# Batch 0's v requested on GpSimd's queue, and batch 1's q transposed on TensorE: one change to a fused attention and MLP kernel

## The chip, the cores and the metric

The kernel runs on one core of a Trainium2 chip. A core has five engines that run side by side: TensorE (PE, with its weight loads as PEld), VectorE (DVE), ScalarE (ACT), GpSimd (POOL) and SyncE (SP), and 16 DMA engines that all queues share. The metric is the device time of one execution in microseconds. Before the change the median of three runs was 294.74 us (294.08 to 295.0).

## The reference

Inputs are q, k and v of 8 batches, 8 heads, 576 positions and 64 features, in float32, and the weights of one MLP.

```python
q_s = softmax(q, axis=-1)              # over the 64 features
k_s = softmax(k, axis=2)               # over the 576 positions
kv  = einsum('bhsd,bhse->bhde', k_s, v)
x   = einsum('bhsd,bhde->bhse', q_s, kv)   # then heads side by side: 4608 x 512
h   = x @ w_in                         # 512 -> 2048
g   = h + sin(alpha * h) ** 2 / alpha
out = g @ w_out                        # 2048 -> 512
```

## The kernel before, in words

Each batch of q, k and v comes as three loads of 128 partitions x 4 x 576 floats, into a pool of five staging buffers (`load`, L85). Partition groups hold even and odd heads; index `ii` (0 or 1) picks two of the four head columns, and a load with `halves=True` is two transfers, one for each `ii`. The 576 positions are 64 groups (partitions) of J = 9 rows j.

For a batch, `exp_q` and `exp_k` (L120, L124) make bfloat16 exponentials on ACT; `norm_q` (L133) sums on DVE and multiplies into the tile qn; `cast_v` makes the bfloat16 v, vb. `kv_mm` (L149) multiplies the transposed k by v, with a column of ones in vb that gives k's sums; `kv_norm` (L162) divides on DVE and writes the block-diagonal weights kbd. q has to be transposed: `q_transpose` (L178) does it on TensorE with an identity, and copies from PSUM; `q_transpose_dma` (L188) does it with DMA transposes from SP. `attn_chunk` (L211) multiplies kbd by the transposed q, and a copy puts the result into xT, the input of the MLP.

The MLP runs over 9 blocks of 512 tokens. For a block, 16 slots `ni` make 128 of the 2048 hidden columns each: `mm_h` (L222) does 4 matmuls into PSUM, `sine` (L238) takes the sine on ACT and squares it on ACT, POOL or DVE, `combine` (L249) writes g on DVE. The output matmuls `mm_o` (L253) follow, 64 for a block; block 0 has its own order, `o_quad` (L354), 64 steps of which the last 16 use the last quarter of w_out. `take(os, n)` emits the next n of them between other work. `evac_o` copies from PSUM and stores.

The order of all instructions on each engine is the order in which the program calls them (`manual_schedule`); a DMA request is an instruction on the engine that issues it, waits there in turn, and goes to that engine's queue (SP, ACT or GpSimd). Transfers that cast float32 weights to bfloat16 (`load_win` L104, `load_wout` L109) go on GpSimd's queue. The kernel holds those back: a copy named held (L317) on GpSimd waits for k's first half, and the requests stand behind it. The first 256 columns of w_in come another way: as float32 on SP's queue into a staging buffer (wf, L278), with two casts on GpSimd (L321).

The head of the program deals with batch 0 by hand: q, k, v and wf are requested on SP in that order (L270 to L280). Between block 0's output matmuls it prepares batch 1 (L398 to L420), with `load_batch(2)` at L406. `late` (L379) is a table of loads that are requested after a given slot of block 0; each load of batch 1 has a DVE copy as a gate.

Of the kernel before, what the change touches and what calls it, by code (L numbers as in the profile page):

```python
# [15 lines left out]
F32 = mybir.dt.float32  # L16
# [7 lines left out]
def kernel(  # L24
# [20 lines left out]
    J = 9  # L45
# [30 lines left out]
    def src_view(t, b):  # L76
        return t[b].rearrange("(i e) (p j) d -> (e p) i (j d)", e=2, j=J)
# [7 lines left out]
    def load(name, t, b, halves=False, eng=nc.sync, gate=None):  # L85

        st = stage.tile([128, 4, J, D], F32, name=f"st_{name}", tag="st")
        for ii in range(2) if gate else ():
            gate(st[:, ii, 0, 0:1], zero)
        view = src_view(t, b)  # L90
        flat = st.rearrange("p i j d -> p i (j d)")
        if halves:
            for ii in range(2):
                eng.dma_start(out=flat[:, ii::2], in_=view[:, ii::2])  # L94
        else:
            eng.dma_start(out=flat, in_=view)
        staged[name, b] = st

    def load_batch(b):
        load("q", q, b)  # L100
        load("k", k, b)
        load("v", v, b)

    def load_win(c0, c1):  # L104
        n = slice(c0, c1)
        for x in range(2):
            nc.gpsimd.dma_start(out=win[64 * x:64 * x + 64, :, n], in_=win_v[x][:, :, n])

    def load_wout(c):  # L109
        nc.gpsimd.dma_start(out=wout[:, 4 * c:4 * c + 4, :], in_=wout_v[:, 4 * c:4 * c + 4, :])  # L110
# [9 lines left out]
    def exp_q(b):  # L120
        A["qe", b] = att2.tile([128, J, 4 * D], BF16, name="qe")
        exp_to(A["qe", b], staged["q", b])

    def exp_k(b):  # L124
        A["ke", b] = att2.tile([128, J, 4 * D], BF16, name="ke")
        exp_to(A["ke", b], staged["k", b])

    def cast_v(b, engs):
        vv = vb[b % 2].rearrange("p j (i c) -> p i j c", i=4)
        for ii in range(2):  # L130
            engs[ii](vv[:, 2 * ii:2 * ii + 2, :, 0:D], staged["v", b][:, ii::2])  # L131

    def norm_q(b, engs):  # L133

        qe = A["qe", b].rearrange("p j (ii x d) -> p ii j x d", ii=2, x=2)
        A["qn", b] = qn = att1.tile([128, 2, J, 2 * D], BF16, name="qn")
        qs = small.tile([128, J, 4], F32, name="qs")
        if len(engs) == 1:
            nc.vector.tensor_reduce(qs, A["qe", b].rearrange("p j (i d) -> p j i d", i=4), axis=AXL.X, op=ALU.add)  # L139
            nc.vector.reciprocal(qs, qs)  # L140
        for ii in range(2):
            part = qs[:, :, 2 * ii:2 * ii + 2]
            if len(engs) == 2:
                nc.vector.tensor_reduce(part, qe[:, ii], axis=AXL.X, op=ALU.add)  # L144
                nc.vector.reciprocal(part, part)
            engs[ii % len(engs)].tensor_tensor(qn[:, ii].rearrange("p j (x d) -> p j x d", x=2), qe[:, ii],  # L146
                                               part.unsqueeze(3).to_broadcast([128, J, 2, D]), op=ALU.mult)

    def kv_mm(b, ii, pool, split=False):  # L149

        if ii == 0 or split:
            A["kvp", b] = pool.tile([128, 2, 512], F32, name="kvp", tag="a")
        kvp, ke, vt = A["kvp", b], A["ke", b], vb[b % 2]
        for j in range(J):
            for e in range(2):
                r = slice(64 * e, 64 * e + 64)
                nc.tensor.matmul(kvp[:, e, ii * 130:(ii + 1) * 130],  # L157
                                 ke[r, j, ii * 128:(ii + 1) * 128],
                                 vt[r, j, ii * 130:(ii + 1) * 130],
                                 start=(j == 0), stop=(j == J - 1))  # L160
# [17 lines left out]
    def q_transpose(b, ii, pool, eng):  # L178
        tp = pool.tile([128, 16, 128], BF16, name="tp", tag="a")
        q_transpose_ii(b, ii, 0, J, tp)  # L180
        eng(q_tile(b)[:, ii], tp[:, 0:J])
# [6 lines left out]
    def q_transpose_dma(b, halves=False):  # L188
        for ii in range(2) if halves else (slice(0, 2),):
            out, in_ = q_tile(b)[:, ii], A["qn", b][:, ii]  # L190
            if not halves:
                out, in_ = out.rearrange("p ii j c -> p (ii j) c"), in_.rearrange("p ii j c -> p ii (j c)")
                in_ = in_.rearrange("p ii c -> p (ii c)")
            else:
                in_ = in_.rearrange("p j c -> p (j c)")
            nc.sync.dma_start(out=out, in_=in_, transpose=True)
# [69 lines left out]

    ACT_CP, DVE_CP, GP_CP = nc.scalar.copy, nc.vector.tensor_copy, nc.gpsimd.tensor_copy
    V, GP = nc.vector, nc.gpsimd
    nc.scalar.dma_start(out=alpha_rows, in_=moe_alpha.rearrange("(no ni) -> no ni", ni=128))
    load("q", q, 0, halves=True)  # L270
    load("k", k, 0, halves=True)
    staged["v", 0] = st = stage.tile([128, 4, J, D], F32, name="st_v", tag="st")
    VJ = ((0, 0, 9), (1, 0, 5), (1, 5, 9))
    for ii, j0, j1 in VJ:
        nc.sync.dma_start(out=st[:, ii::2, j0:j1].rearrange("p i j d -> p i (j d)"),
                          in_=src_view(v, 0)[:, ii::2, j0 * D:j1 * D])

    wf = stage.tile([128, 4, J, D], F32, name="st_w", tag="st")[:, :, 0:4].rearrange("p c a b -> p c (a b)")  # L278
    for x in range(2):
        nc.sync.dma_start(out=wf[64 * x:64 * x + 64], in_=win_v[x][:, :, 0:256])  # L280
    make_identity(nc, ident)
    DVE_CP(identb, ident)
    zero = singles.tile([128, 1], F32, name="zero")
# [13 lines left out]
    DVE_CP(alpha_sb, tpa)  # L297
    nc.vector.reciprocal(inva_sb, alpha_sb)

    exp_q(0)  # L300
    exp_k(0)

# [10 lines left out]
    warm_up(7)  # L313
    norm_q(0, [V, V])
    q_tile(0)

    GP_CP(singles.tile([128, 1], F32, name="held"), staged["k", 0][:, 0, 0, 0:1])  # L317
    for c0, c1 in ((256, 512), (512, 1024), (1024, 1536)):
        load_win(c0, c1)
    for n in range(2):  # L320
        GP_CP(win[:, :, n * 128:n * 128 + 128], wf[:, :, n * 128:n * 128 + 128])  # L321
    load_win(1536, 2048)
    for c in range(2):
        load_wout(c)
    q_transpose_ii(0, 0, 0, 8, tps[0])
    ACT_CP(A["qT", 0][:, 0, 0:8], tps[0])
    cast_v0(0, 0, 5, ACT_CP)
# [39 lines left out]
    def take(it, n=1000):  # L367
        for _ in range(n):
            if next(it, 0) == 0:
                return  # L370
# [4 lines left out]
    with ES:  # L375
        def lent():
            return ps_e.tile([128, 2, MF], F32, name="hh", tag="a")[:, 0]

        late = {6: lambda: load("q", q, 1, halves=True, gate=DVE_CP), 8: lambda: load_wout(2),  # L379
                13: lambda: load("k", k, 1, halves=True, gate=DVE_CP)}  # L380
        for ki in range(2):
            for ni in range(2):
                mm_h(0, ni, lent, ki, ki + 1)
        for ni in range(nN):
            h_slot(0, ni, "DPAPPAPPAPPAPPAP"[ni], lag, lent)
            flush(lag, 1)
            if ni in late:
                late[ni]()
        flush(lag, 0)

        accs = [ps_h.tile([128, dm], F32, name="hp", tag="h") for _ in range(4)]
        os = o_quad(0, accs, [DVE_CP, ACT_CP, DVE_CP, ACT_CP])
        take(os, 20)
        xp = ps_e.tile([128, 4, P], F32, name="xp", tag="a")
        for c in range(4):
            attn_chunk(0, c, 8, 9, xp[:, c])
        DVE_CP(xT[:, :, 8 * P:9 * P], xp)
        take(os, 26)  # L398
        exp_q(1)
        load("v", v, 1, halves=True)  # L400
        norm_q(1, [GP, V])
        load_wout(3)
        exp_k(1)
        cast_v(1, [ACT_CP, DVE_CP])
        q_transpose_dma(1, halves=True)
        load_batch(2)  # L406
        nc.scalar.activation(zero, zero, AX.Sin)
        take(os, 2)
        for ii in range(2):
            kv_mm(1, ii, ps_e, split=True)  # L410
            kv_norm(1, ii, ii + 1)
        take(os, 4)

        c0 = J * P
        for ii in range(2):
            xp = ps_e.tile([128, 2, 512], F32, name="xp", tag="a")[:, :, 0:7 * P]
            for e in range(2):
                attn_chunk(1, 2 * ii + e, 0, 7, xp[:, e])
            (ACT_CP, DVE_CP)[ii](xT[:, 2 * ii:2 * ii + 2, c0:c0 + 7 * P], xp)
            take(os, 2)  # L420
        take(os)
        load("q", q, 3)
        load("k", k, 3)

        for ki in range(2):
            for ni in range(2):
                mm_h(1, ni, lent, ki, ki + 1)
        for ni in range(nN):
            h_slot(1, ni, SQ[ni], lag, lent)
            flush(lag, 1)  # L430
        cast_v(2, [GP_CP, GP_CP])
        flush(lag, 0)
# [134 lines left out]
```

## Time and profile before

| what | value |
|---|---|
| median of the runs | 294.74 us |
| profiled execution | 295.0 us |
| its span | 293.2 us |
| PE, ACT, DVE, POOL busy in the span | 275.7, 226.8, 188.0, 80.1 us |
| granted TensorE clock, mean | 0.993 |
| SP's queue | 42.28 MB, 48.1% of 16 engines' span |
| GpSimd's queue | 3.93 MB, 8.6% |
| first matmul of block 0, of block 1 | 16.29, 52.33 us |

Times in the views count from the start of the span. "Busy" of an engine is the time in its own instructions; a request for a DMA isn't counted. The chain that ended last goes back from the last instruction to whatever released it, step by step, and so shows which waits set the end. The bytes of GpSimd's queue are counted as written, in bfloat16; twice as many are read.

### The profile page before, as it was taken

How to read it: one execution, taken by the hardware profiler on the slowest of the kernel's cores; microseconds unless marked ns; L12 is line 12 of the kernel's file. 1: busy time of each engine (PE TensorE's matmuls, PEld its weight loads, DVE VectorE, ACT ScalarE, POOL GpSimd, SP SyncE). 2: the span in 40 equal slices, each digit the busy share in tenths (PEclk: the TensorE clock that was granted, in tenths of full speed). 3: DMA queues.
4: the chain of work that ended last, by engine and by line, in shares of the span. 5: the costliest groups of instructions: out<-in, count | busy, mean ns of one | idle time of the engine just before them, and what ended most of it. 6: DMA issues, size and time to landing. Idle time of an engine off the chain costs nothing.

```text
span 293.2 us, 4233 instructions
## 1 busy us (share of the span) xinstructions
PE 275.7 (94%) x1552; PEld 130.3 (44%) x1552; DVE 188.0 (64%) x279; ACT 226.8 (77%) x320; POOL 80.1 (27%) x74
## 2 busy tenths in 40 slices
PE   2799976999899999999999999999999999999995
PEld 1434442444445444444544454445444444444443
DVE  3867782599957847774767576766775455555412
ACT  4699862799748999889988998899887777777500
POOL 0678430466386646002420151005000000000000
PEclk9999997999999999999999999999999999999999
DMA  7999979993959986116941693115311111111142
GB/s 255 326 204 246 332 192 271 394 318 100 256 120 319 410 299 122 39 36 190 389 96 36 196 393 85 36 37 78 76 36 38 36 36 38 36 36 37 36 111 72
DMA packets 40261, 46.62 MB, mean 159 GB/s; under 512 B 18336, under 2 KB 23728, under 8 KB 40240
## 3 DMA queue, kind: packets, MB, share of 16 engines
q1 hardware_dynamic: 35760, 42.28, 48.1%
q0 software_dynamic: 4288, 3.93, 8.6%
q8 instruction: 12, 0.20, 0.3%
q10 hardware_dynamic: 192, 0.14, 0.2%
q14 instruction: 9, 0.07, 0.1%
HBM read 36.71 MB, written 9.44 MB: 157 GB/s over the span
## 4 chain that ended last, share of the span: by engine, by line
PE 82%; DMA 7%; DVE 3%; POOL 2%; issue 2%; SPq 1%; ACT 1%; POOLq 0%
PE hp L234 36%; PE op L254 33%; DMA st_w<-in_moe_w_in_dram 3%; PE hp L254 3%; PE hh L234 3%; DMA wout<-in_moe_w_out_dram 2%; PE kvp L157 2%; DMA qT<-qn 2%; PE xp L206 2%; DVE qs L144 1%; PE op L537 1%; PE op L234 1%; POOL s L244 1%; ACT s L240 1%; SPq L94 1%
## 5 line engine op out<-in xcount | busy, mean ns | idle before, releaser
L250 DVE SCALAR_TENSOR_TENSOR g<-s,inva_sb,hp 128x512 bf16<-128x512 f32 x130 | 96.2, 746 | 64.6 <-ACT s L242 54.2
L234 PE MATMUL hp<-xT,win 128*128 128x512 bf16 x520 | 129.9, 379 | 0.2 <-POOL win L321 0.2
L254 PE MATMUL op<-wout,g 128*128 128x512 bf16 x496 | 124.2, 379 | 0.0
L240 ACT ACTIVATE s<-hp,alpha_sb 128x512 f32<-128x512 f32 x130 | 87.7, 682 | 25.4 <-PE hp L234 24.2
L234 PEld LDWEIGHTS <-win 128*128 128x128 bf16 x576 | 56.2, 98 | 67.8 <-POOL win L321 0.9
L254 PEld LDWEIGHTS <-g 128*128 128x128 bf16 x560 | 54.5, 98 | 67.9 <-issue 7.4
L242 ACT ACTIVATE s<-s 128x512 f32<-128x512 f32 x112 | 70.5, 630 | 3.6
L146 POOL TENSOR_TENSOR qn<-qe,qs 128x1152 bf16<-128x1152 bf16 x12 | 25.3, 2128 | 72.3 <-DVE qs L140 62.4
L244 POOL TENSOR_TENSOR s<-s 128x512 f32<-128x512 f32 x29 | 30.5, 1063 | 27.1 <-ACT s L240 25.8
L260 DVE COPY o<-op 128x512 f32<-128x512 f32 (+2 forms) x33 | 22.1, 670 | 10.2 <-PE op L254 7.9
L117 ACT ACTIVATE qe<-st_q 128x1152 bf16<-128x1152 f32 x16 | 17.8, 1155 | 2.6 <-DMA st_q<-in_q_dram 2.5
L117 ACT ACTIVATE ke<-st_k 128x1152 bf16<-128x1152 f32 x16 | 17.9, 1151 | 2.5 <-DMA st_k<-in_k_dram 2.5
L254 PE MATMUL hp<-wout,g 128*128 128x512 bf16 x64 | 15.6, 397 | 4.0 <-DMA wout<-in_moe_w_out_dram 4.0
L139 DVE TENSOR_REDUCE qs<-qe 128x36 f32<-128x2304 bf16 x5 | 12.8, 2553 | 8.7 <-ACT qe L117 8.6
L131 POOL CAST vb<-st_v 128x1152 bf16<-128x1152 f32 x12 | 13.6, 1164 | 12.1 <-DMA st_v<-in_v_dram 7.9
L209 DVE CAST xT<-xp 128x512 bf16<-128x512 f32 (+1 forms) x18 | 13.4, 743 | 0.0
L157 PE MATMUL kvp<-vb,ke 64*128 64x130 bf16 x288 | 9.8, 216 | 0.8 <-ACT vb L310 0.8
L157 PEld LDWEIGHTS <-ke 64*128 64x128 bf16 x288 | 8.2, 93 | 4.1 <-issue 1.8
L117 ACT ACT_TABLE_LOAD x7 | 9.0, 1283 | 1.3 <-PEq L551 1.2
L234 PE MATMUL hh<-xT,win 128*128 128x512 bf16 x40 | 9.4, 379 | 0.0
L144 DVE TENSOR_REDUCE qs<-qe 128x18 f32<-128x1152 bf16 x6 | 8.0, 1330 | 1.9 <-ACT qe L117 1.9
L206 PE MATMUL xp<-qT,kbd 128*128 128x256 bf16 (+1 forms) x40 | 8.2, 286 | 0.4 <-DVE xT L209 0.3
(67 smaller groups left out, 114.6 us busy)
## 6 DMA issues: line engine op xcount, KB each, us to landing
out_dram<-o SPq DMA_DIRECT2D x70, 128.0 KB, 2.4
st_q<-in_q_dram SPq DMA_DIRECT2D x6, 1152.0 KB, 6.3
st_k<-in_k_dram SPq DMA_DIRECT2D x6, 1152.0 KB, 9.0
st_v<-in_v_dram SPq DMA_DIRECT2D x6, 1152.0 KB, 10.2
st_q<-in_q_dram SPq DMA_DIRECT2D x4, 576.0 KB, 5.4
st_k<-in_k_dram SPq DMA_DIRECT2D x4, 576.0 KB, 6.3
wout<-in_moe_w_out_dram POOLq DMA_DIRECT2D x4, 512.0 KB, 8.8
st_v<-in_v_dram SPq DMA_DIRECT2D x3, 576.0 KB, 8.0
```

Source lines behind the costliest of these rows:

```text
L117: nc.scalar.activation(dst[:, :, ii * 128:(ii + 1) * 128].rearrange("p j (x d) -> p x j d", x=2), src[:, ii::2], AX.Exp)
L131: engs[ii](vv[:, 2 * ii:2 * ii + 2, :, 0:D], staged["v", b][:, ii::2])
L146: engs[ii % len(engs)].tensor_tensor(qn[:, ii].rearrange("p j (x d) -> p j x d", x=2), qe[:, ii], part.unsqueeze(3).to_broadcast([128, J, ...
L157: nc.tensor.matmul(kvp[:, e, ii * 130:(ii + 1) * 130], ke[r, j, ii * 128:(ii + 1) * 128], vt[r, j, ii * 130:(ii + 1) * 130], start=(j == 0 ...
L206: nc.tensor.matmul(xp[:, e, 0:n], kt[:, e, ii], qT[:, ii, j0:j1, e * 64:(e + 1) * 64], start=True, stop=True)
L234: nc.tensor.matmul(hp, win[:, ki, ni * 128:(ni + 1) * 128], xT[:, ki, t * MF:(t + 1) * MF], start=(ki == 0), stop=(ki == 3))
L240: nc.scalar.activation(s, hp, AX.Sin, scale=alpha_sb[:, ni:ni + 1])
L242: nc.scalar.activation(s, s, AX.Square)
L244: nc.gpsimd.tensor_tensor(s, s, s, op=ALU.mult)
L250: nc.vector.scalar_tensor_tensor(G[t][:, ni], in0=s, scalar=inva_sb[:, ni:ni + 1], in1=hp, op0=ALU.mult, op1=ALU.add)
L254: nc.tensor.matmul(acc, G[t][:, ni, j * 128:(j + 1) * 128], wout[:, ni, :], start=(ni == 0), stop=(ni == nN - 1))
L260: eng(o[:, cols], acc)
```

## The change

- q of batch 0: the half `ii` = 0 is requested on SP, the half `ii` = 1 on ACT, and alpha's load comes behind that on ACT. k's halves stay on SP.
- The copy held waits for q's first half instead of k's. Behind it GpSimd requests v of batch 0 in the same three pieces, then all of w_in in five pairs (256, 256, 512, 512 and 512 columns), then two quarters of w_out.
- The float32 columns, wf, and their casts on GpSimd are gone.
- The last quarter of w_out is requested after slot 10 of block 0; it was requested after `norm_q(1)`.
- Batch 1's q is transposed on TensorE, with two copies on DVE, in place of two DMA transposes on SP. `load_batch(2)` comes right behind batch 1's v.
- Batch 1's `kv_mm` halves come after 8 and 2 more output matmuls; before they came after 2 more, one directly behind the other, with 4 behind them.

The words that came with the change also say that j 8 of batch 0 comes later; the diff holds nothing on that.

```diff
@@ head @@
+    staged["q", 0] = st = stage.tile([128, 4, J, D], F32, name="st_q", tag="st")
+    for ii, eng in ((0, nc.sync), (1, nc.scalar)):
+        eng.dma_start(out=st.rearrange("p i j d -> p i (j d)")[:, ii::2], in_=src_view(q, 0)[:, ii::2])
     nc.scalar.dma_start(out=alpha_rows, in_=moe_alpha.rearrange("(no ni) -> no ni", ni=128))
-    load("q", q, 0, halves=True)
     load("k", k, 0, halves=True)
-    staged["v", 0] = st = stage.tile([128, 4, J, D], F32, name="st_v", tag="st")
-    VJ = ((0, 0, 9), (1, 0, 5), (1, 5, 9))
-    for ii, j0, j1 in VJ:
-        nc.sync.dma_start(out=st[:, ii::2, j0:j1].rearrange("p i j d -> p i (j d)"),
-                          in_=src_view(v, 0)[:, ii::2, j0 * D:j1 * D])
-
-    wf = stage.tile([128, 4, J, D], F32, name="st_w", tag="st")[:, :, 0:4].rearrange("p c a b -> p c (a b)")
-    for x in range(2):
-        nc.sync.dma_start(out=wf[64 * x:64 * x + 64], in_=win_v[x][:, :, 0:256])
...
+    GP_CP(singles.tile([128, 1], F32, name="held"), staged["q", 0][:, 0, 0, 0:1])
+    staged["v", 0] = st = stage.tile([128, 4, J, D], F32, name="st_v", tag="st")
+    for ii, j0, j1 in ((0, 0, 9), (1, 0, 5), (1, 5, 9)):
+        GP.dma_start(out=st[:, ii::2, j0:j1].rearrange("p i j d -> p i (j d)"),
+                     in_=src_view(v, 0)[:, ii::2, j0 * D:j1 * D])
+    for c0, c1 in ((0, 256), (256, 512), (512, 1024), (1024, 1536), (1536, 2048)):
+        load_win(c0, c1)
+    for c in range(2):
+        load_wout(c)
...
-    GP_CP(singles.tile([128, 1], F32, name="held"), staged["k", 0][:, 0, 0, 0:1])
-    for c0, c1 in ((256, 512), (512, 1024), (1024, 1536)):
-        load_win(c0, c1)
-    for n in range(2):
-        GP_CP(win[:, :, n * 128:n * 128 + 128], wf[:, :, n * 128:n * 128 + 128])
-    load_win(1536, 2048)
-    for c in range(2):
-        load_wout(c)
@@ block 0 and batch 1 @@
         late = {6: lambda: load("q", q, 1, halves=True, gate=DVE_CP), 8: lambda: load_wout(2),
-                13: lambda: load("k", k, 1, halves=True, gate=DVE_CP)}
+                10: lambda: load_wout(3), 13: lambda: load("k", k, 1, halves=True, gate=DVE_CP)}
...
         load("v", v, 1, halves=True)
+        load_batch(2)
         norm_q(1, [GP, V])
-        load_wout(3)
         exp_k(1)
+        for ii in range(2):
+            q_transpose(1, ii, ps_e, DVE_CP)
         cast_v(1, [ACT_CP, DVE_CP])
-        q_transpose_dma(1, halves=True)
-        load_batch(2)
         nc.scalar.activation(zero, zero, AX.Sin)
+        take(os, 8)
+        kv_mm(1, 0, ps_e, split=True)
+        kv_norm(1, 0, 1)
         take(os, 2)
-        for ii in range(2):
-            kv_mm(1, ii, ps_e, split=True)
-            kv_norm(1, ii, ii + 1)
-        take(os, 4)
+        kv_mm(1, 1, ps_e, split=True)
+        kv_norm(1, 1, 2)
+        take(os, 1)
```

## The prediction

> **What bounds the kernel now.** I read the chain that ended last first (page part 4, then in order of time for the first 53 us), then the busy time by stage, then the timeline of the first 20 us, then the DMA requests. Over 82% of the chain is TensorE. What is not TensorE lies in two places that the change touches: before 16.85 us, and between 35 and 52 us.
>
> The chain of waits, in order of time (start, us, what):
> ```profile
> 5.39 10.09 DMA st_w<-in_moe_w_in_dram
> 15.62 1.19 POOL win L321 x2
> 16.85 1.69 PE hp L234 x7
> ...
> 37.25 2.07 POOL qn L146
> 39.32 6.91 DMA wout<-in_moe_w_out_dram
> 46.28 1.28 PE hp L254 x4
> 47.55 0.75 PE xp L214 x2
> 48.30 0.85 PE hp L254 x2
> 49.15 0.75 PE xp L214 x2
> 49.90 2.43 PE hp L254 x10
> 52.33 0.86 PE hp L234 x4
> ```
> The fourth quarter of w_out is requested at 39.32, because the request stands behind qn on GpSimd, and TensorE waits for it until 46.28. After that the matmuls are slow: 2 in 0.85 us at 48.30, where 16 took 3.45 us at 20.26 (0.2157 each).
>
> Busy time by stage (length, then busy of PE, PEld, DVE, ACT, POOL, granted clock, DMA share, GB/s):
> ```profile
> 16.85:30.62 13.77, 13.77 (x64) 6.28 (x65) 9.98 (x17) 13.26 (x22) 11.94 (x14) 1.00 1.21 242
> 30.62:41.03 10.41, 10.41 (x53) 4.61 (x51) 8.34 (x13) 8.77 (x9) 4.54 (x4) 1.00 0.97 291
> 41.03:52.33 11.30, 7.30 (x58) 3.60 (x58) 4.50 (x10) 2.31 (x4) 0.00 (x0) 0.85 1.03 242
> ```
> TensorE is full from 16.85 to 41.03, then has 7.30 us of 11.30, at a clock of 0.85. DVE, ACT and POOL are far from full there.
>
> The timeline of the head (start, us; in brackets the idle time before it and what ended it):
> ```profile
> 4.76 1.16 ACT L117 ACTIVATE qe<-st_q 128x1152 bf16<-128x1152 f32 x1 [2.25 <-DMA st_q<-in_q_dram]
> 5.95 1.35 DVE L144 TENSOR_REDUCE qs<-qe 128x18 f32<-128x1152 bf16 x1 [1.92 <-ACT qe L117]
> 6.17 1.16 ACT L117 ACTIVATE qe<-st_q 128x1152 bf16<-128x1152 f32 x1 [0.26 <-DMA st_q<-in_q_dram]
> 8.23 0.82 POOL L317 COPY held<-st_k 128x1 f32<-128x1 f32 x1 [6.92 <-DMA st_k<-in_k_dram]
> 8.99 4.07 POOL L107 DMA_DIRECT2D win<-in_moe_w_in_dram  x6
> 13.79 0.62 ACT L310 CAST vb<-st_v 128x512 bf16<-128x512 f32 x1 [1.46 <-DMA st_v<-in_v_dram]
> ```
> q's halves land near 4.7 and 6.1, v's last piece near 13.75. DVE's softmax chain (5.95 to 11.96) runs behind the first q half. A request on GpSimd's queue is slow to start: by the packet records, the first w_in data moved at about 13.2, 4.2 us after its request at 8.99; wout's last quarter, alone on the engines, reached its full rate 3.1 us after 39.32.
>
> **Part 1, the head: q on two queues, v and w_in on GpSimd's.** Removed: the two w_in requests on SP (0.75 each) and two casts on POOL (1.19 together, on the path at 15.62). Added: on ACT one q request (about 0.45, ahead of a table load with 2.25 idle behind it: free), and alpha behind it; on POOL three v requests and two more of w_in at about 0.65, with the wait for q in front.
>
> When does q land? Both halves are now asked for at 0.73 and the same 16 engines serve both. Where two queues were busy together, from 42.4 to 45.2 (wout and the transposes), each moved 37 to 40 packets in every 0.25 us, so I take one to one: both halves land at 6.1, the time of the second now. The bounds are 4.7 and 6.1. Then exp starts at 6.1 instead of 4.76, and all of DVE's chain moves by 1.35, from 11.96 to 13.3. alpha lands with q, near 6.3; its small transpose and two DVE operations (0.17 and 0.25) fit before 7.3.
>
> v: held ends at 6.1 + 0.82 = 6.95, data 3.1 to 4.2 later at 10.05 to 11.15 (k is through by 9.6), and 1.18 MB at about 400 GB/s (q's halves landed 1.45 apart, 0.59 MB each) with 0.3 for the last landing: v complete at 13.4 to 14.5, near the 13.75 of now. w_in's first 256 columns follow at 14.8 to 16, no cast behind them.
>
> From 13.3: ten transposes 0.73 (14.05), kvp of the first half 0.6 (14.7), of the second 0.6 (15.3; DVE's two v casts, 1.04, end at 14.25 and ACT's last one at 14.1 to 15.1), kvr and kbd 0.8 each on DVE (15.55, 16.35), the last two attention matmuls 0.61 (17.0), DVE's last xT 0.68 behind its own neighbour (17.75; now 17.10). Five of the 64 matmuls of block 0 are done by then; 59 x 0.2157 = 12.7 more end at 30.5, against 30.62. **Head: -0.1**, between +0.7 (v at the late end) and -1.2 (q's first half at 4.7 as now: the last xT near 16.4, end 29.3).
>
> The Trainium skill (DMA: Bandwidth & Descriptors, Specifications) gives about 1 us as first-byte latency on GpSimd's path. The rows here say 3.1 to 4.2, and the rows decide; with 1 us v would land near 12, and the sum would be the same, DVE's chain being last.
>
> Behind it: w_in's five pairs and w_out's two quarters stand in one queue, 6.3 MB at 400 GB/s. 128 columns come every 0.65 us and are used every 0.86, so block 0 does not starve. POOL's ninth request and those after wait for landings eight back, the last one near 17; POOL's first square comes at 19.5, so 2 us cover that.
>
> **Part 2, w_out's last quarter ten slots earlier.** It is requested after the squares of slots 9 and 10, near 28.9, in place of 39.32. Cost: 0.80 on POOL, whose squares of 12 and 13 come 0.5 later; the accumulators that wait for slot 13 are used 1.7 us into the next stage: at most 0.2. DMA: from 33 on, about 1.55 MB of w_out and 2.36 MB of k and v of batch 1 share 400 GB/s: w_out through by 41, v by 42.8 (now 40.74). That ends the wait of 46.28 - 42.2 = 4.0 us, and the slow clock after it.
>
> **Part 3, batch 1's q transposed on TensorE.** Removed: two DMA transposes that hold SP for 6.37 us and keep batch 2's loads until 45.87. Added: 18 transposes (ten took 0.73: 1.3) and two DVE copies of 128x1152 from PSUM. No row has that copy: ACT's 128x1024 took 0.99 (scaled 1.12), DVE's 128x896 cast from f32 1.09 (scaled 1.40); I take 1.25.
>
> **The stage from 30.62, walked.** TensorE: 46 output matmuls and j 8 until 40.5, as now. qn's halves are ready at 39.4 and 40.6: transposes to 41.85; 8 output matmuls to 43.55; kvp first half 44.15; 2 to 44.6; kvp second 45.2; 1 to 45.4. DVE: two copies 41.2 to 43.7, v cast 0.76 (44.5; v landed at 42.8), o 0.69 (45.2), norms 0.8 each (46.0, 46.8). The second pair of xp, 0.4 at full clock, then ends at 47.25 and five output matmuls at 48.3. Block 1 starts at 48.3 against 52.33: **-4.0**, from -3.4 to -4.6 with the copies at 1.40 and 1.12 and the transfers 1 us late or early. What is late next is DVE's kbd, not DMA.
>
> Batch 2's loads move past the transposes on SP, to about 33, behind v of batch 1 in the same queue. The four output tiles are stored behind them, near 52; their buffers are needed again only at 65. From block 1 on the order is unchanged and everything moves along; the DMA transposes of batch 2 (4.74 us on SP at 74.40) remain.
>
> **Sum.** Span 293.2 - 0.1 - 4.0 = 289.1. The profiled execution took 295.0, 1.8 more than its span: 290.9. It lies 0.26 above the median of the runs, 294.74: **290.6 us**. "j 8 of batch 0 later" is in the words but not in the diff; I cost it at nothing.
>
> **Rivals.**
> (a) q's first half still lands first, at 4.7: the head gains 1.2 in all and the time is 289.4. For it: each half is 16 descriptors for each engine, asked for by SP first. Against: the one-to-one packets above. The Trainium skill (the same page, Queues, rings and completion order) has each engine drain a packet of some 9 to 17 descriptors before it switches, by which this is what would happen; the rows of 42.4 to 45.2 do not show such bursts. Chance 0.13.
> (b) v comes late, 1 to 2 us after 13.75, since its request waits for q and POOL's copy: the head loses 0.7 to 2, 292.0. For it: 4.2 us on the first w_in request. Chance 0.20.
> (c) Slower: GpSimd's queue serves v like its slowest rows. w_in's longest landing was 9.3 us, w_out's 10.9. From 6.95 v's first piece then lands at 16.3 to 17.9, the last 1.5 to 2 later, at 18 to 20, and block 0 starts 4.3 to 6 us late: 294.9 to 296.6. It reaches no change and then decides from v complete at about 18.7, 5 us after now. Against: those rows had a backlog in front, v has none. Chance 0.12, 0.11 of it past the 0.3%.
> (d) The wait moves: batch 1's k and v are pushed back by w_out and kvp waits for them, 1 us for each us that v lands after 43.5. For no change v would have to land near 47.5; 294.5. The rates above leave no room for this. Chance 0.06.
> The forecast, 289.7 to 291.5: 0.49.
>
> **How the numbers follow.** A change of under 0.3% (0.9 us) can't be told from none. Slower is most of (c): 0.11. Same is (d) and the rest of (c): 0.07. Faster is the remainder: 0.82. The range takes in (a), (b) and the milder half of (d), and leaves out (c): 288.6 to 294.0.
>
> **What will show it.** Right: no wait for wout in the chain near 40 to 46; granted clock 1.00 in that stage; block 1's first L234 near 48.3; transposes right behind the 46th output matmul; exp of both q halves back to back from 6.1; first h matmul near 16.5. Wrong: ACT's or DVE's v cast after 15 with TensorE idle before kvp; TensorE waiting on win or on ke or vb of batch 1; clock below 1.00 in block 0.

## The result, and the profile after

| what | before | after |
|---|---|---|
| median of the runs compared, us | 294.87 (294.08 to 295.08, 4 runs) | 289.62 (289.56 to 289.95, 4 runs) |
| profiled execution, its span, us | 295.0, 293.2 | 289.56, 287.8 |
| block 0's first h matmul (L234), in the timeline | 16.29 | 16.79 |
| block 1's start (first long L234 piece of the chain) | 52.33 | 48.42 |
| from there to the end of the span | 240.9 | 239.4 |
| mean granted TensorE clock | 0.993 | 1.00 |

The ratio is 0.9829, with a 95% interval of 0.9809 to 0.9849: the changed kernel takes 1.7% less. Of the 5.4 us that the span loses, 3.9 lie ahead of block 1 and 1.5 behind it.

The chain of waits of the changed kernel, in order of time (start, us, what):

```profile
1.27 5.18 DMA alpha_rows<-in_moe_alpha_dram
...
7.08 0.25 DVE inva_sb L291
7.33 1.22 DVE qs L144
...
13.25 0.73 PE tp L186 x10
13.98 0.64 PE kvp L157 x18
...
33.27 10.52 DMA st_v<-in_v_dram
43.81 0.76 DVE vb L131
...
45.30 0.28 DVE kbd L170
45.60 0.30 DVE kbd L170
45.95 0.55 PE xp L214 x2
46.50 0.43 PE hp L254 x2
...
48.42 3.45 PE hp L234 x16
...
72.02 3.84 DMA qT<-qn
```

wout is gone from it. What stands there now is the second half of batch 1's v, which was requested at 33.27 and landed at 43.79; behind it come DVE's cast, its kbd and the last matmuls of block 0, at the granted clock of 1.00 (2 L254 in 0.43, against 0.85 before). The head of the chain begins with alpha's load, not with q: it comes behind q's second half on ACT's queue, and DVE's two operations on alpha end at 7.33, where DVE's first sum of q starts.

Busy time by stage of the changed kernel (length, then busy of PE, PEld, DVE, ACT, POOL, granted clock, DMA share, GB/s):

```profile
16.85:30.62 13.77, 13.77 (x65) 6.17 (x64) 10.17 (x17) 13.41 (x22) 9.68 (x11) 1.00 1.20 240
30.62:41.03 10.41, 10.39 (x54) 4.73 (x53) 8.34 (x12) 5.99 (x8) 4.50 (x4) 1.00 1.14 302
41.03:48.42 7.39, 7.32 (x78) 3.89 (x76) 5.25 (x12) 5.21 (x6) 0.00 (x0) 1.00 1.04 408
```

The stage that had 7.30 us of TensorE work in 11.30 us, at a clock of 0.85, now has 7.32 in 7.39, at 1.00. The DMA engines are as full in it as before by their share (1.04 against 1.03), but they move 408 GB/s in place of 242.

The timeline of the changed kernel (start, us; in brackets the idle time before it and what ended it):

```profile
5.80 2.22 ACT L117 ACTIVATE qe<-st_q 128x1152 bf16<-128x1152 f32 x2 [2.71 <-DMA st_q<-in_q_dram]
5.83 0.19 POOL L294 COPY held<-st_q 128x1 f32<-128x1 f32 x1 [4.51 <-DMA st_q<-in_q_dram]
5.95 2.32 POOL L297 DMA_DIRECT2D st_v<-in_v_dram  x3
...
13.25 0.73 PE L186 MATMUL tp<-identb,qn 128*128 128x128 bf16 x10 [0.67 <-DVE qn L146]
...
40.89 1.17 PE L186 MATMUL tp<-identb,qn 128*128 128x128 bf16 x18
41.59 1.42 DVE L181 COPY qT<-tp 128x1152 bf16<-128x1152 bf16 x2 [0.61 <-PE tp L186]
...
43.81 0.76 DVE L131 CAST vb<-st_v 128x1152 bf16<-128x1152 f32 x1 [0.80 <-DMA st_v<-in_v_dram]
```

q's two halves land at 5.77 (SP) and 6.23 (ACT), and exp of both runs back to back from 5.80. TensorE's transposes at 13.25 wait for DVE's qn, not for v. In batch 1, the two copies from PSUM take 1.42 us together, and then DVE stands for 0.80 us until v is there.

### The profile page after: what moved, and what is told of

Its sections match the earlier page's. It is cut to its first block, busy times and chain, and to the rows that moved or that the text cites. A ratio compares the mean times of both kernels' runs of the same rounds, so it can differ in the third digit from the quotient of the medians.

```text
span 287.8 us, 4258 instructions
## 1 busy us (share of the span) xinstructions
PE 275.4 (96%) x1570; PEld 130.8 (45%) x1570; DVE 188.6 (66%) x281; ACT 226.5 (79%) x320; POOL 81.7 (28%) x77
## 4 chain that ended last, share of the span: by engine, by line
PE 76%; DMA 7%; DVE 6%; ACT 4%; POOL 3%; issue 2%; ACTq 0%; SPq 0%; POOLq 0%
PE hp L234 34%; PE op L254 33%; DMA st_v<-in_v_dram 4%; POOL s L244 3%; ACT s L240 3%; PE kvp L157 2%; DMA alpha_rows<-in_moe_alpha_dram 2%; DVE qs L144 2%; PE xp L206 2%; DMA qT<-qn 1%; PE op L534 1%; PE op L234 1%; PE hh L234 1%; DVE qn L146 1%; DVE o L260 1%
## 5 line engine op out<-in xcount | busy, mean ns | idle before, releaser
L234 PE MATMUL hp<-xT,win 128*128 128x512 bf16 x520 | 129.8, 379 | 0.0
L254 PE MATMUL op<-wout,g 128*128 128x512 bf16 x496 | 124.2, 379 | 0.0
L234 PEld LDWEIGHTS <-win 128*128 128x128 bf16 x576 | 56.2, 98 | 67.4 <-issue 0.4
L254 PEld LDWEIGHTS <-g 128*128 128x128 bf16 x560 | 54.1, 98 | 61.7 <-issue 0.9
L254 PE MATMUL hp<-wout,g 128*128 128x512 bf16 x64 | 15.1, 379 | 0.0
L209 DVE CAST xT<-xp 128x512 bf16<-128x512 f32 (+1 forms) x18 | 13.4, 743 | 0.0
L234 PE MATMUL hh<-xT,win 128*128 128x512 bf16 x40 | 9.4, 379 | 0.0
```

What stands on the lines that cost most here:

```text
L234: nc.tensor.matmul(hp, win[:, ki, ni * 128:(ni + 1) * 128], xT[:, ki, t * MF:(t + 1) * MF], start=(ki == 0), stop=(ki == 3))
L254: nc.tensor.matmul(acc, G[t][:, ni, j * 128:(j + 1) * 128], wout[:, ni, :], start=(ni == 0), stop=(ni == nN - 1))
```

## The experiments

The kernel before varies more from run to run than the changed one: over the chips of the experiments its runs that are compared went from 293.56 to 297.90, those of the changed kernel from 289.42 to 290.64. Each ratio below is against runs of the kernel before on the same chip, and stands with its 95% interval; it is the measure to go by, since a difference from the median of all runs before on the chip can be off from it by more than 1 us.

**1. The head alone** (q on two queues, v and all of w_in on GpSimd's queue, no float32 columns; nothing else changed).

```diff
+    for ii, eng in ((0, nc.sync), (1, nc.scalar)):
+        eng.dma_start(out=st.rearrange("p i j d -> p i (j d)")[:, ii::2], in_=src_view(q, 0)[:, ii::2])
...
+    GP_CP(singles.tile([128, 1], F32, name="held"), staged["q", 0][:, 0, 0, 0:1])
+    for ii, j0, j1 in ((0, 0, 9), (1, 0, 5), (1, 5, 9)):
+        GP.dma_start(...)
```

> The head alone on the kernel before (q on two queues, v and w_in on GpSimd's). Theory: the head is worth nothing: q's first half lands a microsecond late and DVE's chain with it, the missing f32 columns and casts give that back. First output matmul of block 0 between 30.4 and 30.8 (before 30.46), time 294.4 to 295.2. Rival: the head carries 1 us or more of the gain, 293.9 or less.

Measured: 295.04 us (294.44 to 297.4), ratio 0.9988 [0.9944, 1.0032]. The head alone is worth nothing that can be measured, as the theory said, and the first output matmul of block 0 came at 30.58, inside the 30.4 to 30.8 expected. Its profiled execution was its slowest one (297.4), so its terms say less; the excess was not in the head: the chain there shows batch 1's DMA transposes at 9.57 us from 39.53.

**2. w_out alone** (the last quarter requested after slot 10; the DMA transposes stay).

```diff
-                13: lambda: load("k", k, 1, halves=True, gate=DVE_CP)}
+                10: lambda: load_wout(3), 13: lambda: load("k", k, 1, halves=True, gate=DVE_CP)}
...
-        load_wout(3)
```

> The last quarter of w_out requested after slot 10 and nothing else changed; DMA transposes kept. Theory: the wait for w_out (4.0 us) and the slow clock go, but w_out pushes batch 1's v to about 43.7, and the transposes land near 45 to 46; block 1 starts at 49.2 to 49.6, time 291.8 to 292.3. Rival 1: the request's place is the whole gain of the middle, block 1 at 48.4, 290.9. Rival 2: the DMA transposes hold the stage as long as w_out did, gain under 1.5 us, 293.4 or more.

Measured: 293.55 us (292.75 to 294.98), ratio 0.9892 [0.9819, 0.9965]. By the ratio that is 3.2 us gained, with an interval of 1.0 to 5.3; against the median of all runs before on that chip (295.21) it is 1.7. The time is that of the second rival (293.4 or more), but the chain holds v of batch 1 and kvp, not the DMA transposes. Block 1 starts at 51.49, against 52.33 before and 49.2 to 49.6 expected. The timeline and then the stage, of the kernel with this edit alone:

```profile
38.19 1.16 ACT L117 ACTIVATE ke<-st_k 128x1152 bf16<-128x1152 f32 x1 [3.09 <-DMA st_k<-in_k_dram]
40.49 1.16 ACT L117 ACTIVATE ke<-st_k 128x1152 bf16<-128x1152 f32 x1 [1.14 <-DMA st_k<-in_k_dram]
41.77 1.17 ACT L131 CAST vb<-st_v 128x1152 bf16<-128x1152 f32 x1
42.99 2.21 PE L157 MATMUL kvp<-vb,ke 64*128 64x130 bf16 x36 [2.78 <-ACT vb L131]
```

```profile
41.03:51.49 10.46, 8.28 (x56) 4.36 (x57) 4.76 (x10) 4.77 (x6) 0.00 (x0) 0.67 1.15 299
```

The wait on wout is gone, and another has come in its place: w_out's transfer now runs beside k of batch 1, ACT waits 3.09 and 1.14 us for k, and TensorE stands 2.78 us before kvp, which comes directly behind two output matmuls. The clock falls to 0.67. The changed kernel covers the same wait with TensorE work: its 18 transposes (1.17) and 8 output matmuls (1.89) stand ahead of kvp.

**3. TensorE transposes alone** (with the new order and batch 2's loads early; w_out stays late).

```diff
         load("v", v, 1, halves=True)
+        load_batch(2)
         norm_q(1, [GP, V])
         load_wout(3)
         exp_k(1)
+        for ii in range(2):
+            q_transpose(1, ii, ps_e, DVE_CP)
         cast_v(1, [ACT_CP, DVE_CP])
-        q_transpose_dma(1, halves=True)
-        load_batch(2)
...
```

> Batch 1's q transposed on TensorE, the loads of batch 2 and the order of the output matmuls as in the change, but the last quarter of w_out still requested behind qn on GpSimd, near 39.3. Theory: TensorE stops at the third of the eight output matmuls until w_out lands near 45; block 1 starts near 50.5, time 292.5 to 293.5. Rival: the transposes are what mattered, block 1 at 48.4 to 49, 290.9 to 291.5.

Measured: 298.25 us (297.59 to 298.85), ratio 1.0077 [1.004, 1.0114]: slower than before by 0.8%, against the expectation's sign. The chain of this kernel:

```profile
38.83 10.37 DMA wout<-in_moe_w_out_dram
...
57.25 3.45 PE hp L234 x16
```

w_out's last quarter, requested at the same time as before, takes 10.37 us to land in place of 6.91, and block 1 starts 4.9 us later. By the order of requests it is batch 2's loads, 3.5 MB that are now asked for ahead of it, that share the engines with it. That is a reading until something else is held fixed, so:

**4. The same, with batch 2's loads held back** behind a DVE copy until about 43 us.

```diff
-        load_batch(2)
...
+        load("q", q, 2, gate=DVE_CP)
+        load("k", k, 2)
+        load("v", v, 2)
```

> The kernel of the third experiment (q of batch 1 transposed on TensorE, w_out's last quarter still requested behind qn) with the loads of batch 2 held by a DVE copy behind v's cast, near 43.7, so that they don't share the engines with w_out. Theory: those loads are what made w_out take 10.4 us from its request and that kernel slower than before; here w_out lands near 45, block 1 starts at 50.5 to 51.5, time 291.5 to 293.0. Rival: w_out is as late without them, block 1 near 57, 297.5 or more.

Measured: 293.0 us (291.13 to 293.42) against 295.66, ratio 0.9891 [0.9848, 0.9934], at the upper end of what was expected. The chain:

```profile
38.81 5.80 DMA wout<-in_moe_w_out_dram
44.65 2.72 PE hp L254 x6
...
52.07 3.45 PE hp L234 x16
```

w_out lands 4.6 us sooner, and block 1 starts 5.2 us sooner. So it was batch 2's early loads that made experiment 3 slow, not the transposes on TensorE. The parts don't add: by the ratios, the head alone gives -0.4 us, w_out early -3.2, and the transposes with batch 2's early loads +2.3 (each known to 1.1 to 2.2 us either way), a sum of -1.3 where all three together gave -5.0. As these runs read, the early loads do no harm once w_out is ahead of them, and w_out's early transfer costs nothing once TensorE has work ahead of kvp.

**5. q of batch 0 on one queue**, in the changed kernel: both halves on SP, alpha first on ACT. (These are two changes: q's second half moves, and alpha no longer waits behind it.)

```diff
+    nc.scalar.dma_start(out=alpha_rows, ...)
-    for ii, eng in ((0, nc.sync), (1, nc.scalar)):
+    for ii, eng in ((0, nc.sync), (1, nc.sync)):
```

> The changed kernel with both halves of q on SP, alpha alone on ACT. Theory: exp of the first half starts at 4.7 in place of 5.8, DVE's chain (7.25 to 13.2) ends about 1.0 earlier and block 0 with it: 288.4 to 288.9. Rival 1: v, requested a microsecond earlier, then takes k's share and k is late: no change, 289.4 to 289.9. Rival 2: v or w_in's first columns bind at once, gain under 0.5.

Measured: 288.98 us (288.75 to 289.39), ratio 0.9737 [0.9684, 0.979]. In its profile v of batch 0, landed at 13.25, was the last thing ahead of kvp. To compare it with the changed kernel itself, both were run again on another chip, with one more edit beside them (experiment 6).

> The changed kernel as it is, timed beside the variants on one chip: 289.4 to 290.0.

> The changed kernel with q's halves both on SP, again, beside the changed kernel on one chip. Theory from its first profile: block 0 starts 1.0 earlier, but v of batch 1 lands only 0.4 earlier and block 1 starts 0.4 earlier; 0.3 to 0.7 faster than the changed kernel. Rival: the difference of the first run was between chips, under 0.2.

Measured there: the changed kernel 289.86 (289.42 to 290.64), q on one queue 289.13 (289.04 to 289.34), 0.73 less. The chain of the kernel with q on one queue:

```profile
0.74 3.99 DMA st_q<-in_q_dram
4.75 1.17 ACT qe L117
...
15.71 1.78 PE hp L234 x8
...
32.05 11.30 DMA st_v<-in_v_dram
43.38 0.76 DVE vb L131
...
47.98 3.45 PE hp L234 x16
```

The first exp starts at 4.75 in place of 5.68, and block 0's h matmuls at 15.71 in place of 16.77 in the changed kernel's run beside it. Of that 1.06, some 0.2 is alpha's: in the changed kernel the first exp ended at 6.84, but DVE began its sum at 7.06, behind its two operations on alpha. At block 1 only 0.6 of the 1.06 is left (47.98 against 48.62): v of batch 1 was requested 1.0 us earlier but landed at 43.35 against 44.00, and in both kernels the DMA engines move 404 to 414 GB/s from 39 us on. So the two choices, q's second half on ACT and alpha behind it, cost the change 0.7 us, and the middle of the kernel takes back part of what an earlier head gives. The Trainium skill (DMA: Bandwidth & Descriptors, Issuing engines are not separate DMA queues) says that DMAs from different engines run on the same 16 DMA engines, and that issuing from several saves only issue time. This agrees: asked for on two queues the halves landed at 5.65 and 6.06, asked for on one at 4.73 and 6.22, so that the second gains 0.16 us and the first loses 0.92. ACT is busy with the first half for 1.16 us, so the earlier second half is of no use to it.

**6. v of batch 0 back on SP**, behind k, in the changed kernel; q stays on two queues.

```diff
     load("k", k, 0, halves=True)
+    staged["v", 0] = ...
+    for ii, j0, j1 in ((0, 0, 9), (1, 0, 5), (1, 5, 9)):
+        nc.sync.dma_start(...)
```

> The changed kernel with v of batch 0 back on SP's queue, behind k; w_in stays on GpSimd's, requested as q's first half lands. Theory: DVE's chain binds block 0 (last xT near 17.7), v and w_in's first columns both land before they are needed, so v's queue is worth nothing: within 0.4 of the changed kernel. Rival: w_in's casting transfers now share the engines with k and v, v's last piece lands after 14 and block 0 starts 0.5 to 1.5 late, 290.1 or more.

Measured: 289.37 us (289.21 to 289.5), 0.49 under the changed kernel on that chip (289.86), a little more than the 0.4 within which it was expected. The chain:

```profile
16.86 1.78 PE hp L234 x8
...
48.04 3.45 PE hp L234 x16
```

ACT's last cast of v starts 0.9 us later than on GpSimd's queue (13.77, against 12.85 in the changed kernel on that chip), and still just in time: the h matmuls start at 16.86 against 16.77, so the head is the same. The gain is in the middle, where v of batch 1 is no longer in the chain and block 1 starts at 48.04. GpSimd's queue then carries weights alone from the start, and w_in was requested first at 5.85 (8.13 in the changed kernel on that chip). The last quarter of w_out landed at 38.33 in place of 40.67, and v of batch 1 at 43.12 in place of 44.00, though requested 0.2 later. So the weights are through earlier; that this is what speeds v up fits with experiment 2, where w_out's transfer made v late, but wasn't tested by itself.

**7. Both of these together.**

> Both small gains at once, on the changed kernel: q's two halves both on SP (alpha first on ACT), and v of batch 0 on SP behind k, with only weights on GpSimd's queue. Theory (the two gains have different places, so they add in part): the first exp starts near 4.75 instead of 5.70 to 5.80, v lands near 13.8 to 14.4 since nothing but w_in is beside it, the h matmuls start at 15.9 to 16.4 (16.77 in the changed kernel, 15.71 with q alone on SP, 16.86 with v alone on SP), batch 1's v is out of the chain as it is with v alone on SP, and block 1 starts at 47.1 to 47.6 (48.04 with v alone). With an unchanged tail of 239.5: 288.3 to 288.9 us, under both single edits (289.13 and 289.37). Rival 1 (batch 1's v is bound by the 16 DMA engines whenever block 0 starts earlier): the chain holds st_v of batch 1 again, block 1 starts near 48.0, 289.0 to 289.4. Rival 2 (the weights on GpSimd's queue, now asked for 1 us earlier beside k and v, push v's last piece to 15 or later): the h matmuls start at 16.8 or later and the time is 289.3 or more.

Measured: 290.17 us (289.54 to 293.34) against 296.41 of that chip, ratio 0.9811 [0.9769, 0.9852], no better than either edit alone (0.9777 and 0.9783, on another chip). The chain:

```profile
4.82 9.83 DMA st_v<-in_v_dram
14.67 0.64 ACT vb L314
15.35 0.42 PE kvp L157 x8
...
17.26 1.78 PE hp L234 x8
...
48.45 3.45 PE hp L234 x16
```

The second rival came in the main: with the weights asked for at 5.58, beside k and v, the last piece of v lands at 14.65 where 13.8 to 14.4 was expected, and kvp waits for it; the h matmuls start at 17.26. That either edit works because of slack that the other one uses up fits with this. But q was late as well in this profile, its first half at 5.41 where 4.73 was measured with q alone on SP, and no run shows why.

**8. What became shorter behind block 1.** The 1.5 us there were not in the prediction at all. In both kernels, SP's queue at that place holds two output stores, v of batch 3 and then batch 2's DMA transposes. SP's timeline in the kernel before:

```profile
70.58 1.86 SPq L263 DMA_DIRECT2D out_dram<-o  x2
72.54 0.53 SPq L96 DMA_DIRECT2D st_v<-in_v_dram  x1
74.40 4.74 SPq L196 DMA_TRANSPOSE qT<-qn  x2
```

and in the changed kernel:

```profile
66.66 1.11 SPq L263 DMA_DIRECT2D out_dram<-o  x2
67.88 0.54 SPq L96 DMA_DIRECT2D st_v<-in_v_dram  x1
70.53 3.39 SPq L196 DMA_TRANSPOSE qT<-qn  x2
```

The two stores take 0.75 us more at issue before, and the transposes 1.35 more. Two short stretches of the DMA packets, 70.9 to 71.3 us of the kernel before and then 62.9 to 63.4 us of the changed one (queue, packets, MB, share of 16 engines):

```profile
q8 instruction: 1, 0.02, 15.6%
```

```profile
q8 instruction: 1, 0.02, 17.1%
```

These are single transfers of 16 KB on the queue "instruction". The first starts at 71.07, on top of the second store's request (71.10, which took 1.35 us by itself); the second starts at 63.22 of the changed kernel, where SP issues nothing. The changed kernel has 18 more transposes, 36 rows of TensorE with their weight loads, ahead of this place; its transfer comes 3.4 us ahead of the first of the two stores and not on top of the second. To test whether this is the cause, 18 pairs of small PE instructions were put into the head of the kernel before (experiment 8a), which moves the transfer off, and 200 PE instructions into the head of the changed kernel (8b), which moves one to 69.0; and a control (8c) has the 84 of these that lie in the warm-up, and its transfers at 59.4 and 77.4.

```diff
@@ 8a: before @@
+    for _ in range(18):
+        nc.tensor.matmul(warm[:, 1, 0:16], identb, identb[:, 0:16], start=True, stop=True)
@@ 8b: after; 8c: the same without this loop @@
+    for _ in range(58):
+        nc.tensor.matmul(warm[:, 1, 0:16], identb, identb[:, 0:16], start=True, stop=True)
...
-            nc.tensor.matmul(warm, identb, A["qe", 0][:, 0:4, 0:128], start=True, stop=True)
+            nc.tensor.matmul(warm[:, 0], identb, A["qe", 0][:, 0, 0:128], start=True, stop=True)
...
-    warm_up(7)
+    warm_up(29)
...
-    warm_up(6)
+    warm_up(26)
```

> The kernel before with 18 pairs of a weight load and a 16-column matmul added at the start of TensorE, where it waits for alpha anyway: 36 more instructions, as many as the change adds, and no work moved. Theory: the 16 KB instruction fetch that fell on SP's request at 71.1 us (1.35 us for a request that takes 0.60) moves some 4 us earlier relative to the program, v of batch 3 is requested 0.75 earlier and the DMA transposes of batch 2 end 0.7 to 1.5 earlier: 293.4 to 294.2. Rival: the 1.5 us that the change gained behind block 1 come from its own loads, and this changes nothing, 294.6 to 295.1.

> The changed kernel with 200 more TensorE instructions in the head, in its idle time and in place of the warm-up matmuls (same length, 128 columns each): the instruction fetch moves by some 15 us, onto SP's requests near 67. Theory: a request there takes 1.3 in place of 0.6, and the DMA transposes of batch 2 end 0.7 to 1.5 later: 290.3 to 291.1. Rival: no change, 289.4 to 289.9.

> Control for the 200 added instructions: the same 128-column warm-up matmuls but without the 58 pairs ahead, 84 more TensorE instructions than the changed kernel. The instruction fetch of 63 falls near 56 and the next near 75, neither on SP's requests and loads from 66.5 to 73.8. Theory: 289.4 to 290.0, block 1 to the end 239.2 to 239.7. Rival: it was the changed warm-up that cost 1.1 there, and this costs as much, 290.5 or more.

Measured: 8a 295.76 us (295.21 to 298.74), ratio 1.0031 [1.0003, 1.0059], so 0.9 us slower where 0.7 to 1.5 less was expected. 8b 290.75 (290.51 to 291.3), ratio 0.9852 [0.9824, 0.9879], as expected. 8c 290.1 (289.56 to 290.81), beside 289.86 for the changed kernel on that chip, just over the 290.0 expected. By its total, then, 8a missed, and 8b and 8c were timed on different chips. The tail, from block 1's start to the end, can be read from the profiles apart from what lies ahead of it. Worked out from the spans, block 1's start in the chain, and the packet records:

```
kernel                  16 KB transfer at   what it fell on                    tail, us
before                  71.1                2nd store's request (1.35 us)      240.9
exp. 1 (head)           73.3                2nd store's request (1.61 us)      241.0
exp. 2 (w_out)          70.2                2nd store's request (1.23 us)      240.7
8b (200 more)           69.0                v of batch 3 in flight             240.8
after                   63.2                nothing (request 0.60 us)          239.4
exp. 3 (transposes)     71.9                before the store at 76.0 (0.60)    239.4
exp. 4 (loads held)     66.7                before the store at 70.8 (0.60)    239.6
8a (before, 36 more)    71.7                before the store at 75.9 (0.60)    239.8
8c (control)            59.4, 77.4          nothing until the transposes end   239.8
exp. 5, 6, 7            62.7 to 63.3        nothing (0.60)                     239.3 to 239.6
```

Where the transfer meets the store's request, or v of batch 3 behind it, the rest of the kernel takes 240.7 to 241.0 us; elsewhere 239.3 to 239.8. 8b puts it back into the changed kernel, where v took 7.24 us from its request to its landing in place of 5.78, and its chain shows what that costs, the transposes:

```profile
71.93 5.12 DMA qT<-qn
```

against 3.84 at 72.02. On SP they took 4.74 in 8b and, at the same place, 3.59 in the control 8c:

```profile
70.31 4.74 SPq L196 DMA_TRANSPOSE qT<-qn  x2
70.47 3.59 SPq L196 DMA_TRANSPOSE qT<-qn  x2
```

In 8c the transfer at 77.4 met another store, whose request took 1.31 us as well, where nothing waited for it. Each tail is that of one profile, and how one transfer of 16 KB holds up a request or a load for so long isn't shown.

8a gained 1.0 us in the tail but lost it ahead of block 1. In its profiled execution, the slowest of its runs, batch 1's transposes took 11.70 us from 39.82, with one of these transfers among them at 48.3. They took 9.57 in experiment 1 and 7.64 in the kernel before. Whether the transfer is what made them long, or how they share the engines with w_out, wasn't separated. It stays open why the kernels with batch 1's DMA transposes vary so much from run to run.

## Why the prediction came out

The time, 289.62, is 1.0 under the forecast of 290.6, inside the range of 288.6 to 294.0 and 0.1 under the forecast's own 289.7 to 291.5. Step by step:

- **q's landing: right in the main.** One to one packets put both halves at 6.1; they landed at 5.77 and 6.23, and both exps run from 5.80. From 3 to 5 us the two queues moved 186 and 168 packets. SP's half was first by 0.46, and its packets had begun at 1.85, ACT's at 3.06. Rival (a), the first half at 4.7 as now, did not come. By the Trainium skill (DMA: Bandwidth & Descriptors, Queues, rings and completion order) a DMA engine drains a whole packet of one queue before it switches to the next. By that rule rival (a) would have come; it did not show itself here. Experiment 5 shows about what rival (a) would have given, 0.7 us, alpha's share included.
- **v on GpSimd's queue: too late by 1 to 2 us, without effect.** The forecast had held at 0.82 and data 3.1 to 4.2 us behind the request, v complete at 13.4 to 14.5. held took 0.19 (the row of 0.82 was no price for the copy), the requests began at 5.95, and by the packet records v's data moved from 8.4 on, 2.4 us behind the request, and was complete at 12.57. The other profiles with v on this queue had it complete at 12.4 to 14.1, so the forecast's range was within what happens. v's first data came at 8.2 to 8.4 in all seven of them, whether it was asked for at 4.9 (experiment 5) or at 5.8 to 5.95, so 2.4 to 3.4 us behind. w_in's came 4.0 to 4.2 behind (experiments 6 and 7, and the kernel before), and those of w_out's last quarter before 1.5 behind, at 40.85. So the delay is no fixed price of the queue, nor of the cast, since w_out casts too; what sets it stays open. Rivals (b) and (c), which rested on v coming late, did not come.
- **DVE's softmax chain last in the head: right, but not for the reason given.** 13.3 was forecast for its end, and the transposes started at 13.25. Its start was to be the end of the first exp; that came at 6.96, 0.3 sooner than forecast, but DVE was then held until 7.33 by its two operations on alpha, which the forecast had as done by 7.3 and off the path. The two errors cancel. kbd ended at 16.30 (16.35), the last xT at 17.68 (17.75). Block 0's first h matmul came at 16.79 in place of 16.5, its first output matmul at 30.66 against 30.46 before. So the head cost 0.2 in place of the -0.1 forecast; in experiment 1 it could not be told from nothing.
- **The wait for w_out, and the clock: right.** No wait for wout, clock 1.00, and all of TensorE's 46 matmuls by 40.89 (40.5).
- **The middle, 4.0: right in sum, by two errors that cancel.** The copies from PSUM were taken at 1.25 us each, with bounds of 1.12 and 1.40. They take 0.75 each (1.42 for both): 1.1 us too much. v of batch 1 was taken to land at 42.8 and landed at 43.8: 1.0 too little. Its request went out at 33.27, 0.66 later than before. The remaining 0.3 is the sharing with w_out, which was taken as too cheap, and not batch 2's loads behind v on SP's queue: v took 8.32 us to land with them and w_out late (experiment 3), 8.44 without them (experiment 4), 11.15 with w_out early and batch 2 late (experiment 2), and 10.52 in the changed kernel. So what is late next is v and not DVE alone, as the forecast had it. That is the beginning of rival (d): v landed 0.3 us past the 43.5 from which (d) counts, and DVE stood 0.80 for it. The copy was priced by a cast from float32 (128x896 in 1.09, so 1.22 ns for an element in each partition); from bfloat16 it is 0.65 ns, about half. The Trainium skill (VectorE: DVE Perf Modes, Why PSUM operands drop a tier) says just this: a PSUM operand allows the doubled rate at most, and float32 none. The rows agree with that ratio.
- **"From block 1 on the order is unchanged and everything moves along": wrong.** This is the step that failed. The order is unchanged but the tail is 1.5 us shorter; the profiles of experiment 8 put that down to the place of a 16 KB transfer on the instruction queue. The miss is small beside the stated range, and the rest came out within 0.1, itself with errors that cancel, so the time was right all the same. Span forecast 289.1, + 0.1 at block 1, - 1.5 behind it: 287.7, measured 287.8.

"j 8 of batch 0 later" was costed at nothing, and no row after shows a difference there.

## What to carry to other kernels

The parts of a change can be worth little or less than nothing one by one and much together: a transfer moved early helps in full only when whatever it pushes back is covered, so look in the stage's DMA share and in the wait behind the one you remove. When the DMA engines are full in a stage, part of what is saved ahead of it can be lost there again (0.4 of 1.06 us in experiment 5). A small load behind a large one on a queue can hold up an engine (alpha's, by 0.2 to 0.3 us here): follow the chain to its first step. Price an operation by a row of its own input type: bfloat16 from PSUM was half of float32.

## What the runs showed of the hardware

- A transfer of 16 KB on the instruction queue (12 in the kernel before, 0.20 MB) comes at a place that goes by the number of TensorE's instructions: 36 more of them in the head brought it forward from the second store's request to 4.2 us ahead of it (8a). A store request on SP that it met took 1.23 to 1.61 us in place of 0.60, in four kernels of the table; with batch 2's DMA transposes close behind, the tail became 0.9 to 1.7 us longer. Not every request that it meets is held up: with one at 45.87 in the changed kernel, the requests at 45.81 and 46.48 took 0.58 and 0.65.
- A request on SP can take long to issue when much is queued ahead of it: k and v of batch 2 took 3.29 and 2.80 us, at about 410 GB/s on the engines from 39 us on; in the kernel before 0.49 and 0.46.
- A load was not delayed by the loads queued behind it on SP's queue, but by a transfer on GpSimd's queue: the second half of batch 1's v took 8.32 us to land with batch 2's loads behind it (experiment 3), 8.44 without them (experiment 4), and 11.15 with w_out's last quarter beside it (experiment 2).
- On GpSimd's queue the first data moved 1.5 to 4.2 us behind the first request: 2.4 to 3.4 for v, without a cast; 4.0 to 4.2 for w_in, with one; 1.5 for w_out's last quarter in the kernel before, with one.
- With DMA transposes beside w_out's transfer, the first half of the same transposes took 7.64, 9.57 and 11.70 us in three profiles of kernels with the same order there (before, experiment 1, 8a); the runs of one kernel on one chip lie 0.3 to 1.3 us apart with TensorE transposes (2.3 and 3.8 in experiments 4 and 7) and 1.0 to 4.3 apart with DMA transposes.
